# Two fused MoE layers behind block attention: token tiles scaled a step after they are summed, an early activation for the first slice of layer two, and a last slice finished on VectorE

## The chip, the cores and the metric

The kernel runs on one core of one Trainium2 chip. The metric is the device time of one execution in microseconds. The profile shows one such execution on five engines: PE (TensorE, matrix products; PEld is its weight load), DVE (VectorE), ACT (ScalarE), POOL (GpSimd) and SP, whose queue issues every transfer of this kernel.

## The reference

```python
attn = softmax(q k^T / 8, masked by blocks of 64) @ v     # 4 x 8 heads, 576 tokens, 64 wide
x = attn as 2304 tokens x 512
h = x @ w_in;   g = h * clip(h + 3, 0, 6) / 6;   x = g @ w_out          # layer one: 512 -> 2048 -> 512
h = x @ w_in2;  g = h * tanh(softplus(h));       out = g @ w_out2       # layer two
```

Everything is in single precision. The kernel makes each product of three matrix products over a high and a low part of its operands (high x high, high x low, low x high), so every operand of TensorE is first split in two.

## The kernel before, in words

**Stages.** Attention comes first, over 16 pairs of heads. Then the two layers run as one list of 160 steps, `steps` (L806): layer `m` (0, 1), token block `j` (four of 512 tokens and one of 256), slice `f` (16 slices of 128 of the 2048 inner columns). Step n makes slice n. Block 0 of layer one is steps 0 to 15, block 1 begins at step 16; layer two begins at step 80; the last slice is step 159. Below, "in 12" is `ff_in` of slice 12 (12 matmuls, L275 to L277), "out 12" is `ff_out` of slice 12 (12 matmuls, L773 to L775), and so on for other operations.

**Order.** The schedule is manual: each engine runs its instructions in the order in which the Python loop at L916 calls the stages, and waits only where its data or a buffer is not ready. In step n the loop runs through the three lists of `MOE_PLAN` (L60): list 0 for steps of block 0, list 1 for the other steps of layer one, list 2 for layer two. An entry `("out", 2)` means that step n calls out of slice n - 2.

**One slice of layer one.** `in` writes h in PSUM (two buffers); `act_a` (ACT L285) takes relu(h + 3); `act_c3` (DVE L331) multiplies by h and so frees h; `act_gh` (ACT L349) rounds the result to its high part gh; `act_gl` (POOL L356) subtracts to get the low part gl; `out` uses gh (L773, L775) and gl (L774). In layer two the activation is longer: `a` (ACT L287), `b1` (DVE L294), `b2` (DVE L301), `ln` (ACT L306), `c3` (DVE L336), `rexp` (ACT L314), `c1` (DVE L318), `c2` (DVE L324), `mul` (POOL L343), `gh`, `gl`.

**Token tiles.** Each block's input comes in four tiles k = 0 to 3 of 128 x 512. For layer one, `load_x` (L224) issues on SP: raw (`xr`, two buffers), low (`xs`, one buffer), rs (`xn`, one buffer, two transfers). Then `add_x` sums raw and low (POOL L245), `mul_x` scales by rs (DVE L250), and `split_x` makes the high part xh (ACT L257) and the low part xl (DVE L262), after which raw's buffer is free. The steps in which these run, counted from the block's first step, are the tuples `XLOAD`, `XADD` and `XSPLIT` at L102: their first entry is for block 1, the second for the later blocks of layer one, the third for layer two. `xa`, `xm`, `xh`, `xl` and `dma` are their places in a plan.

**Beside it in block 0.** Up to step 13 the weights of the later slices are still being converted: per step two rebases on ACT (L163), two signs on POOL (L168), two merges L182 and two L185 on DVE, two copies on ACT (L202), and one subtraction on POOL and one on DVE (L207).

**The turns.** At step 80 the outs of layer one's last slices (256 tokens) are called at lag 2 and those of layer two at lag 3, so TensorE's order is in 80, out 79, in 81, in 82, in 83, out 80, in 84, out 81. At the end it is out 158, out 159, then `evacuate` and the last stores.

Of the kernel before, what the change touches and what calls it, by code (L numbers as in the profile page):

```python
# [25 lines left out]
FT = DFF // P  # L26
# [4 lines left out]
BLOCKS = [(t, min(512, NT - t)) for t in range(0, NT, 512)]  # L31
# [28 lines left out]
MOE_PLAN = (  # L60
    (
        ("evac", 3), ("c3", 1), ("w0", 0), ("w1", 0), ("gh", 1), ("gl", 1), ("xh", 0), ("in", 0),
        ("w2", 0), ("w3", 0), ("a", 0), ("out", 2), ("whi", 0), ("dma", 0), ("wlo", 0), ("xl", 0),
        ("xa", 0), ("xm", 0),
    ),
    (
        ("evac", 3), ("c3", 1), ("gh", 1), ("gl", 1), ("xh", 0), ("w0", 0), ("in", 0), ("out", 2),
        ("w1", 0), ("w2", 0), ("w3", 0), ("xl", 0), ("a", 0), ("whi", 0), ("dma", 0), ("wlo", 0),
        ("xa", 0), ("xm", 0),
    ),  # L70
    (
        ("evac", 4), ("in", 0), ("out", 3), ("a", 0), ("gh", 2), ("gl", 2), ("b1", 0), ("b2", 0),
# [26 lines left out]
RELOAD = 4  # L99


XLOAD = (-7, -4, -3, -2), (-11, -9, -6, -3), (-11, -9, -9, -6)  # L102
XADD = (-5, -4, -3, -2), (-10, -8, -5, -2)
XSPLIT = (-4, -3, -2, -1), (-9, -7, -4, -1), (-10, -8, -7, -1)
END = 0


def f32(ap):
    return ap.bitcast(F32)
# [7 lines left out]
def fused_kernel(ctx: ExitStack, tc: tile.TileContext, qT, kT, vv, w1, w2, outT):  # L117
    nc = tc.nc
# [147 lines left out]
    ht, et, qt, rt, gt = {}, {}, {}, {}, {}  # L266
# [73 lines left out]
    def act_mul(m, j, f):  # L340
        if m == 1:
            g, _ = gt[m, j, f]
            nc.gpsimd.tensor_mul(g, g, et.pop((m, j, f)))  # L343

    def act_gh(m, j, f):
        n = BLOCKS[j][1]
# [5 lines left out]
    def act_gl(m, j, f):  # L352
        n = BLOCKS[j][1]
        g, gh = gt[m, j, f]
        gl = m3.tile([P, 512], F32R, tag="gl", name=f"gl{m}_{j}_{f}")[:, :n]
        nc.gpsimd.tensor_sub(gl, g, f32(gh))  # L356
        gt[m, j, f] = gh, gl


    with ExitStack() as late:  # L360
# [271 lines left out]
        def stage(fn):  # L632
            def run(g):
                if 0 <= g < NG:
                    fn(g // 5, TIME[g % 5])
            return run

        def stage_v(fn):

            def run(g):  # L640
                p, c = divmod(g - 5, 5)
                if 0 <= p < NP and c < 4:
                    fn(p, c // 2, c % 2)
            return run

        def stage_sums(t):
            def run(g):
                p, s = divmod(g, 5)
                if 0 <= p < NP and s == 4:
                    sums(p, t)  # L650
            return run

        def stage_q(t):
            def run(g):
                p, s = divmod(g, 5)
                if 0 <= p < NP - 1 and s == t:
                    split_q(p + 1, t)
            return run
# [36 lines left out]
        def stage_fetch(g):  # L695
# [4 lines left out]
        stages = dict(  # L700
            load=stage_load, loadv=stage_load_v, T=stage(transposes), hi=stage(keep_hi), lo=stage(keep_lo),
            max=stage(maxima), exp=stage(exps),
            rg=stage_sums(0), rt=stage_sums(1), rc=stage_sums(2), rd=stage_sums(3),
            S=stage(scores), V=stage_v(attn_v), x=stage_v(keep_x), store=stage_v(store_x),
            qh=stage_q(0), ql=stage_q(1), qd=stage_q(2), pool=stage_pool, w=stage_w, fetch=stage_fetch,
        )


        begun = set()
        conv0 = {}  # L710

        def run_early(name, f, *args):
            if name == "load":
                load_x(0, 0, f)
            elif name == "add":
                add_x(0, 0, f)
            elif name == "mul":
                mul_x(0, 0, f)
            elif name in ("xh", "xl"):
                split_x(0, 0, f, name == "xl")  # L720
            elif name == "fetch":
                fetch1(f, *args)
            elif name == "conv":
                c, i = args
                if i == 0:
                    conv0[f, c] = weights1(f, c)
                next(conv0[f, c], None)
            else:
                begun.add((name, f))
                fn = dict(a=act_a, c3=act_c3, gh=act_gh, gl=act_gl)  # L730
                fn["in"] = ff_in
                fn[name](0, 0, f)
# [52 lines left out]
    def put(d, n, *call):  # L785
        d.setdefault(n, []).append(call)
# [15 lines left out]
            dst = x2d[d] if m == 0 else outT[d * P:(d + 1) * P]  # L802
            put(results, now[0], nc.sync.dma_start, dst[:, t0:t0 + n], o)

    NJ = len(BLOCKS)
    steps = [(m, j, f) for m in range(2) for j in range(NJ) for f in range(FT)]  # L806

    conv, dmas, stores, loads, results = {}, {}, {}, {}, {}  # L810
    xs = {}, {}, {}, {}
# [29 lines left out]
    for n, (m, j, f) in enumerate(steps):  # L841
        if m == 0 and j == 0 and f >= WMID:
            for c in range(2):
                put(conv, n - 3, weights1_psum, f, c)
                put(dmas, max(n - AHEAD, 0), fetch1, f, c, True)
        if m == 0 and 1 <= j <= 2:
            i = (j - 1) * FT + f
            put(dmas, n - 2, fetch2, i)
            put(conv, n, narrow2, i)
        if (m, j) == (0, NJ - 1):  # L850
            put(dmas, n + RELOAD, reload2, f)
        if f == 0 and n:
            when = 2 if m else min(j - 1, 1)
            for k in range(KT):
                put(loads, n + XLOAD[when][k], load_x, m, j, k)
                i = n + XSPLIT[when][k]
                if m == 0:
                    put(xs[0], n + XADD[when][k], add_x, m, j, k)
                    put(xs[3], n + XADD[when][k], mul_x, m, j, k)
                put(xs[1], i, split_x, m, j, k, 0)  # L860
                put(xs[2], i, split_x, m, j, k, 1)

    now = [0]
    active = {}

    def group(n):
# [9 lines left out]
    def calls(*ds):  # L876
        def run_stage(n, m):
            if m == group(n):
                for d in ds:
                    for fn, *args in d.pop(n, ()):  # L880
                        fn(*args)
        return run_stage
# [7 lines left out]
    def conv_step(i):  # L890
        def run_stage(n, m):
            if m != group(n):
                return
            if m == 0:
                todo = begin(n) if i == 0 else active.get(n - (i == 5), ())
            elif i == 1:
                todo = begin(n + 1)
            else:
                if i == 0 and n not in active:
                    for x in begin(n):  # L900
                        next(x)
                todo = active[n]
            for x in todo:
                next(x, None)
        return run_stage

    stages = dict(
        a=stage(act_a), b1=stage(act_b1), b2=stage(act_b2), ln=stage(act_ln),
        rexp=stage(act_rexp), mul=stage(act_mul), c1=stage(act_c1), c2=stage(act_c2),
        c3=stage(act_c3), gh=stage(act_gh), gl=stage(act_gl), evac=stage(evacuate),  # L910
        out=stage(ff_out), dma=calls(results, stores, dmas, loads), xa=calls(xs[0]), xh=calls(xs[1]), xl=calls(xs[2]), xm=calls(xs[3]),
        w0=conv_step(0), w1=conv_step(1), w2=conv_step(2), w3=conv_step(3),
        whi=conv_step(4), wlo=conv_step(5),
    )
    stages["in"] = stage(ff_in)
    for n in range(len(steps) + 6):  # L916
        now[0] = n
        for i, plan in enumerate(MOE_PLAN):
            for name, lag in plan:
                if (name, n - lag) not in begun:  # L920
                    stages[name](n - lag, i)
    assert not (dmas or loads or results or stores or conv or any(xs))


# [37 lines left out]
```

## Time and profile before

| | us |
|---|---|
| median of 3 runs (1016.84 to 1017.82) | 1017.66 |
| the profiled execution | 1016.85 |
| its span in the profile | 1014.3 |
| TensorE busy in the span | 985.6 |

The median is 0.81 us above the profiled execution. The span leaves 2.55 us of that execution outside. Times of single instructions below are counted from the start of the span. A row of a timeline reads: start, duration, engine and line, operation, output<-input, shape, and in brackets how long the engine stood idle just before and what ended that.

### The profile page before, as it was taken

To read this page: it belongs to the slowest core of one execution; us is meant where nothing else is said; L and a number is where in the kernel's file an instruction comes from. 1 tells how busy PE (TensorE), PEld (TensorE's weight loads), DVE (VectorE), ACT (ScalarE), POOL (GpSimd) and SP (SyncE) were. 2 spreads that over 40 slices of the span, in tenths; PEclk is the share of its full clock that TensorE was granted. 3 is DMA by queue.
4 is the path that set the end of the run, shared out by engine and by line. 5 is a ranking of instruction groups with operands and counts; after the bars stand their busy time and mean duration, and the time that the engine had idled before them with its cause. 6 is when DMAs were issued, how large, how long until landed. Compare 5 with 4: busy or idle time off the path is not lost.

```text
span 1014.3 us, 14797 instructions
## 1 busy us (share of the span) xinstructions
PE 985.6 (97%) x5184; PEld 842.9 (83%) x5184; DVE 618.7 (61%) x1039; ACT 517.0 (51%) x1175; POOL 583.5 (58%) x510
## 2 busy tenths in 40 slices
PE   6999999989989999999999999999999999999998
PEld 5888899868768888888888997888888888888897
DVE  6888877958856556654222226556656566656575
ACT  4788888846535445444222334445444444444454
POOL 7555544568967787776222223655555565555644
PEclk9999999999999999999999999999999999999999
DMA  6677677788037677674110595000200100100010
GB/s 177 171 200 207 174 187 193 195 284 334 14 112 262 231 256 254 212 248 156 63 31 11 211 392 186 22 1 1 73 11 1 63 21 1 41 18 6 1 42 21
DMA packets 95641, 128.89 MB, mean 127 GB/s; under 512 B 42320, under 2 KB 54608, under 8 KB 95568
## 3 DMA queue, kind: packets, MB, share of 16 engines
q1 hardware_dynamic: 95568, 127.96, 39.5%
q8 instruction: 40, 0.66, 0.3%
q14 instruction: 33, 0.27, 0.1%
HBM read 83.36 MB, written 35.73 MB: 117 GB/s over the span
## 4 chain that ended last, share of the span: by engine, by line
PE 75%; POOL 9%; issue 5%; DVE 4%; DMA 4%; ACT 3%; SPq 1%; POOLq 0%; DVEq 0%; ACTq 0%
PE y L774 11%; PE y L775 11%; PE h L276 11%; PE h L277 11%; PE h L275 11%; PE y L773 11%; PE o L606 3%; POOL gl L356 3%; PE t L576 2%; POOL wl L207 2%; PE s L503 2%; DMA qb<-qs 1%; PE s L504 1%; PE s L505 1%; POOL hq L343 1%
## 5 line engine op out<-in xcount | busy, mean ns | idle before, releaser
L275 PE MATMUL h<-xh,wh 128*128 128x512 f32 (+1 forms) x640 | 237.0, 370 | 4.9 <-DVE e L331 3.0
L774 PE MATMUL y<-gl,wh 128*128 128x512 f32 (+1 forms) x640 | 236.0, 369 | 2.9 <-POOL gl L356 2.9
L277 PE MATMUL h<-xh,wl 128*128 128x512 f32 (+1 forms) x640 | 236.4, 369 | 1.3 <-POOL wl L207 1.3
L773 PE MATMUL y<-gh,wh 128*128 128x512 f32 (+1 forms) x640 | 235.8, 368 | 0.7 <-ACT gh L349 0.7
L276 PE MATMUL h<-xl,wh 128*128 128x512 f32 (+1 forms) x640 | 236.0, 369 | 0.4 <-DVE xl L262 0.4
L775 PE MATMUL y<-gh,wl 128*128 128x512 f32 (+1 forms) x640 | 235.4, 368 | 0.0
L356 POOL TENSOR_TENSOR gl<-e,gh 128x512 fp32r<-128x512 f32 (+1 forms) x80 | 105.5, 1319 | 135.0 <-ACT gh L349 69.9
L356 POOL TENSOR_TENSOR gl<-hq,gh 128x512 fp32r<-128x512 f32 (+1 forms) x80 | 127.6, 1595 | 89.7 <-ACT gh L349 89.7
L343 POOL TENSOR_TENSOR hq<-hq,e 128x512 f32<-128x512 f32 (+1 forms) x80 | 99.3, 1241 | 83.4 <-DVE e L324 82.8
L275 PEld LDWEIGHTS h<-xh,wh 128*128 128x128 f32 x640 | 121.0, 189 | 27.3 <-DVE e L331 3.8
L774 PEld LDWEIGHTS y<-gl,wh 128*128 128x128 f32 x640 | 120.6, 188 | 23.9 <-POOL gl L356 4.2
L277 PEld LDWEIGHTS h<-xh,wl 128*128 128x128 f32 x640 | 121.0, 189 | 21.7 <-POOL wl L207 1.8
L773 PEld LDWEIGHTS y<-gh,wh 128*128 128x128 f32 x640 | 120.7, 189 | 21.6 <-ACT gh L349 1.7
L276 PEld LDWEIGHTS h<-xl,wh 128*128 128x128 f32 x640 | 121.2, 189 | 20.8 <-DVE xl L262 0.6
L775 PEld LDWEIGHTS y<-gh,wl 128*128 128x128 f32 x640 | 120.7, 189 | 19.9
L294 DVE TENSOR_SCALAR e<-e 128x512 f32<-128x512 f32 (+1 forms) x80 | 33.2, 415 | 144.5 <-ACT e L287 136.6
L287 ACT ACTIVATE e<-h 128x512 f32<-128x512 f32 (+1 forms) x80 | 44.4, 555 | 144.9 <-PE h L277 144.9
L331 DVE SCALAR_TENSOR_TENSOR e<-e,h 128x512 f32<-128x512 f32 (+1 forms) x80 | 50.3, 628 | 84.2 <-ACT e L285 83.9
L285 ACT ACTIVATE e<-h 128x512 f32<-128x512 f32 (+1 forms) x80 | 43.8, 548 | 105.7 <-PE h L277 105.7
L349 ACT ACTIVATE gh<-e 128x512 fp32r<-128x512 f32 (+1 forms) x80 | 46.9, 588 | 82.9 <-DVE e L331 82.9
L587 DVE TENSOR_TENSOR t<-t,t 128x512 fp32r<-128x512 f32 (+2 forms) x144 | 69.9, 522 | 26.9 <-ACT t L582 26.7
L536 ACT ACTIVATE p<-s,nm 128x64 f32<-128x64 f32 (+2 forms) x144 | 75.2, 530 | 11.9 <-DVE nm L525 11.9
(63 smaller groups left out, 1621.9 us busy)
## 6 DMA issues: line engine op xcount, KB each, us to landing
raw<-w SPq DMA_DIRECT2D x64, 512.0 KB
x1d<-x SPq DMA_DIRECT2D x64, 144.0 KB
qb<-qs SPq DMA_DIRECT2D x30, 288.0 KB
w2d<-m SPq DMA_DIRECT2D x32, 256.0 KB
w2d<-v SPq DMA_DIRECT2D x32, 256.0 KB
wh<-w2d SPq DMA_DIRECT2D x16, 512.0 KB
wl<-w2d SPq DMA_DIRECT2D x16, 512.0 KB
q<-qT SPq DMA_DIRECT2D x16, 288.0 KB
```

The source lines that it names most:

```text
L275: nc.tensor.matmul(h[:, :n], hi[:, ws], xh, start=(k == 0), stop=False)
L276: nc.tensor.matmul(h[:, :n], hi[:, ws], xl, start=False, stop=False)
L277: nc.tensor.matmul(h[:, :n], lo[:, ws], xh, start=False, stop=(k == KT - 1))
L331: nc.vector.scalar_tensor_tensor(g, g, 6.0, h, op0=ALU.min, op1=ALU.mult)
L343: nc.gpsimd.tensor_mul(g, g, et.pop((m, j, f)))
L349: nc.scalar.activation(gh, g, AF.Copy)
L356: nc.gpsimd.tensor_sub(gl, g, f32(gh))
L536: nc.scalar.activation(t, sc, AF.Exp, bias=nm[:, c:c + 1], accum_out=su[:, i:i + 1])
L587: nc.vector.tensor_sub(z[:, 1, loc, :], tp, f32(z[:, 0, loc, :]))
L773: nc.tensor.matmul(y, hi[:, ws], gh, start=first, stop=False)
L774: nc.tensor.matmul(y, hi[:, ws], gl, start=False, stop=False)
L775: nc.tensor.matmul(y, lo[:, ws], gh, start=False, stop=last)
```

## The change

Three things. For layer one, `mul_x` of a token tile is called one step after its `add_x`, from a place in the middle of the plan (ahead of `dma`) in place of its end; with that the steps of loads, sums and splits move: for block 1 the loads of tiles 1 to 3 and all four sums come a step earlier, so that the scalings stay at steps 11 to 14; for blocks 2 to 4 the sums of tiles 0 to 2 stay, tile 3 is loaded and summed a step earlier, and tiles 0 to 2 are split a step later. Slice 80, the first of layer two, has c1, c2 and mul at the end of step 80 in place of step 81, and gh and gl at the end of step 81 in place of step 82. Slice 159, the last, has mul and gl on VectorE in place of GpSimd.

```diff
@@ MOE_PLAN, list 0
-        ("w2", 0), ("w3", 0), ("a", 0), ("out", 2), ("whi", 0), ("dma", 0), ("wlo", 0), ("xl", 0),
-        ("xa", 0), ("xm", 0),
+        ("w2", 0), ("w3", 0), ("a", 0), ("out", 2), ("whi", 0), ("xm", 0), ("dma", 0), ("wlo", 0),
+        ("xl", 0), ("xa", 0),
@@ MOE_PLAN, list 1
-        ("w1", 0), ("w2", 0), ("w3", 0), ("xl", 0), ("a", 0), ("whi", 0), ("dma", 0), ("wlo", 0),
-        ("xa", 0), ("xm", 0),
+        ("w1", 0), ("w2", 0), ("w3", 0), ("xm", 0), ("xl", 0), ("a", 0), ("whi", 0), ("dma", 0),
+        ("wlo", 0), ("xa", 0),
@@
-XLOAD = (-7, -4, -3, -2), (-11, -9, -6, -3), (-11, -9, -9, -6)
-XADD = (-5, -4, -3, -2), (-10, -8, -5, -2)
-XSPLIT = (-4, -3, -2, -1), (-9, -7, -4, -1), (-10, -8, -7, -1)
+XLOAD = (-7, -5, -4, -3), (-11, -9, -6, -4), (-11, -9, -9, -6)
+XADD = (-6, -5, -4, -3), (-10, -8, -5, -3)
+XSPLIT = (-4, -3, -2, -1), (-8, -6, -3, -1), (-10, -8, -7, -1)
@@ act_mul (and act_gl in the same way)
-            nc.gpsimd.tensor_mul(g, g, et.pop((m, j, f)))
+            eng = nc.vector if (m, j, f) == steps[-1] else nc.gpsimd
+            eng.tensor_mul(g, g, et.pop((m, j, f)))
@@
-                    put(xs[3], n + XADD[when][k], mul_x, m, j, k)
+                    put(xs[3], n + XADD[when][k] + 1, mul_x, m, j, k)
@@ at the end of each step of the loop; first = NJ * FT = 80
+        for name in (("c1", "c2", "mul"), ("gh", "gl"))[n - first] if 0 <= n - first < 2 else ():
+            stages[name](first, 2)
+            begun.add((name, first))
```

## Rows read from the trace of the kernel before

**Rows 1.** The page's part 1: busy time of each engine, share, instructions.

```profile
PE 985.6 (97%) x5184; PEld 842.9 (83%) x5184; DVE 618.7 (61%) x1039; ACT 517.0 (51%) x1175; POOL 583.5 (58%) x510
```

**Rows 2.** Busy time by stretch: length; PE, PEld, DVE, ACT, POOL; clock, DMA, GB/s.

```profile
270.00:302.00 32.00, 28.61 (x122) 22.12 (x121) 19.22 (x25) 12.84 (x24) 22.31 (x18) 1.00 0.32 99
302.00:500.00 198.00, 198.00 (x875) 163.97 (x874) 111.25 (x123) 87.11 (x151) 138.26 (x109) 1.00 0.64 215
600.00:626.00 26.00, 24.70 (x151) 21.48 (x150) 12.11 (x21) 10.15 (x20) 6.22 (x7) 1.00 0.64 235
1003.00:1014.30 11.30, 6.36 (x45) 5.35 (x43) 3.50 (x9) 2.82 (x7) 3.80 (x6) 0.96 0.14 46
```

**Rows 3.** Timeline, steps 12 to 16: a tile's sum, its scaling, c3 12, TensorE.

```profile
281.88 1.74 POOL L245 TENSOR_TENSOR xr<-xr,xs 128x512 f32<-128x512 f32 x1
283.65 0.69 DVE L250 TENSOR_TENSOR xr<-xr,xn 128x512 f32<-128x512 f32 x1 [1.18 <-POOL xr L245]
284.26 0.68 DVE L331 SCALAR_TENSOR_TENSOR e<-e,h 128x512 f32<-128x512 f32 x1
284.99 0.50 PE L275 MATMUL h<-xh,wh 128*128 128x512 f32 x1 [1.44 <-DVE e L331]
...
298.41 0.50 PE L774 MATMUL y<-gl,wh 128*128 128x512 f32 x1 [0.91 <-POOL gl L356]
...
301.08 0.39 PE L275 MATMUL h<-xh,wh 128*128 128x512 f32 x1
```

**Rows 4.** Timeline, step 10: VectorE's two merges L182 beside GpSimd's gl 9.

```profile
264.89 2.83 DVE L182 SCALAR_TENSOR_TENSOR v<-raw,v 128x512 uint32<-128x512 uint32 x2 [1.34 <-POOL v L168]
265.43 1.75 POOL L356 TENSOR_TENSOR gl<-e,gh 128x512 fp32r<-128x512 f32 x1
```

**Rows 5.** Timeline and one stretch: loads, what frees their buffer, when they land.

```profile
191.86 0.33 SPq L233 DMA_DIRECT2D xs<-x1d  x1
194.88 1.27 POOL L245 TENSOR_TENSOR xr<-xr,xs 128x512 f32<-128x512 f32 x1 [1.16 <-DMA xs<-x1d]
...
276.03 0.33 SPq L233 DMA_DIRECT2D xs<-x1d  x1
276.90:278.20 1.30, 0.80 (x4) 0.34 (x3) 1.30 (x3) 0.41 (x1) 0.77 (x1) 1.00 0.65 200
280.68 1.78 DVE L262 TENSOR_TENSOR xl<-xr,xh 128x512 fp32r<-128x512 f32 x1
282.49 0.33 SPq L232 DMA_DIRECT2D xr<-x1d  x1
285.68 1.29 POOL L356 TENSOR_TENSOR gl<-e,gh 128x512 fp32r<-128x512 f32 x1 [2.07 <-ACT gh L349]
```

**Rows 6.** Timeline, the turn to layer two: b1 81, mul 80, b1 82, out 80, gl 81.

```profile
617.41 0.43 DVE L294 TENSOR_SCALAR e<-e 128x512 f32<-128x512 f32 x1 [2.31 <-ACT e L287]
620.68 1.29 POOL L343 TENSOR_TENSOR hq<-hq,e 128x512 f32<-128x512 f32 x1 [11.61 <-DVE e L324]
621.18 1.07 DVE L294 TENSOR_SCALAR e<-e 128x512 f32<-128x512 f32 x1
622.70 0.50 PE L773 MATMUL y<-gh,wh 128*128 128x512 f32 x1 [0.32 <-ACT gh L349]
624.18 0.50 PE L774 MATMUL y<-gl,wh 128*128 128x512 f32 x1 [0.98 <-POOL gl L356]
627.26 1.30 POOL L356 TENSOR_TENSOR gl<-hq,gh 128x512 fp32r<-128x512 f32 x1 [0.74 <-ACT gh L349]
```

**Rows 7.** Timeline, the end: xl at 256 columns, c2 159, gl 158, out 159.

```profile
954.50 0.42 DVE L262 TENSOR_TENSOR xl<-xr,xh 128x256 fp32r<-128x256 f32 x1
1005.46 0.42 DVE L324 SCALAR_TENSOR_TENSOR e<-e,r 128x256 f32<-128x256 f32 x1
1006.44 0.72 POOL L356 TENSOR_TENSOR gl<-hq,gh 128x256 fp32r<-128x256 f32 x1 [0.53 <-ACT gh L349]
1009.17 0.39 PE L774 MATMUL y<-gl,wh 128*128 128x256 f32 x1 [0.25 <-POOL gl L356]
```

More of the change, by code (lines that the diff above doesn't have):

```diff
@@ L355, in act_gl @@
         gl = m3.tile([P, 512], F32R, tag="gl", name=f"gl{m}_{j}_{f}")[:, :n]
-        nc.gpsimd.tensor_sub(gl, g, f32(gh))
+        eng = nc.vector if (m, j, f) == steps[-1] else nc.gpsimd
+        eng.tensor_sub(gl, g, f32(gh))
         gt[m, j, f] = gh, gl
+    NJ = len(BLOCKS)
+    steps = [(m, j, f) for m in range(2) for j in range(NJ) for f in range(FT)]
     with ExitStack() as late:
@@ L803, in evacuate @@
             put(results, now[0], nc.sync.dma_start, dst[:, t0:t0 + n], o)
-    NJ = len(BLOCKS)
-    steps = [(m, j, f) for m in range(2) for j in range(NJ) for f in range(FT)]
     conv, dmas, stores, loads, results = {}, {}, {}, {}, {}
@@ L863, in fused_kernel @@
     now = [0]
+    first = NJ * FT
     active = {}
```

## The prediction, made before the change was run

> **What bounds the kernel now.** I read the page first: TensorE is busy for 97% of the span [rows 1], so only its gaps can be won, and a new gap is paid in full. The busy time by stretch shows where the gaps are [rows 2]. From 302 to 500 us, which holds the token tiles of blocks 2 to 4, TensorE has none: 875 matmuls in 198 us, 0.226 us each. Whatever the new order does for VectorE's waits there is worth nothing as long as it makes no gap. Three stretches have gaps that the change can reach. Steps 11 to 16 (270 to 302 us) hold 122 matmuls, 27.6 us of work at that pitch in 32 us: 4.4 us lost. The turn to layer two (600 to 626 us) has 1.3 us idle; the matmul starts say more: 0.32 us waited ahead of out 80, then 1.48 us between its first two starts where 0.23 is usual, and each matmul after a wait runs 0.1 us longer [rows 6], together 1.8 us. The last 11.3 us hold 45 matmuls, but most of that is the final stores, which stay.
>
> Next the timeline of steps 12 to 16 [rows 3]. The loss there is one pattern, seen four times: VectorE stands still for a sum on GpSimd (until 283.65), scales, and only then does c3, which frees the buffer that the next slice waits for (TensorE starts at 284.99 after 1.44 us). The change takes the scaling away from this place. The question is what comes late next.
>
> **Part one, block 1's token tiles.** Instructions are neither added nor removed: four sums on GpSimd and the loads of tiles 1 to 3 come a step earlier; the scalings stay in steps 11 to 14, but ahead of the step's L207 and xl.
>
> *Steps 10 to 12.* GpSimd and VectorE get in each other's way here: beside GpSimd's gl, two merges L182 take 2.83 us, with one run before gl and the other after it, and gl itself takes 1.75 us, where it takes 1.29 alone [rows 4, 5]. So the sum that now comes in step 10, ahead of step 11's weight conversions, pushes both engines: 1.27 us for the sum [rows 5]. In step 12 gl 11 comes to lie between the two merges, as in [rows 4] (0.6 us, the second merge's wait, net of what it waited before), and the scaling of tile 1 now runs ahead of xl 0 (0.69 us). xl 0, which ends at 282.46 now (280.68 and 1.78), ends some 2.5 us later, at about 284.9. Bounds: not later at all (if the earlier sum fits in a gap), and 3 us.
>
> *The load that is held.* Raw has two buffers, so raw 2 can't be loaded before xl 0 is through: SP issues it at 282.49, 0.03 us after xl 0 [rows 5]. Before, sum 2 stands one step after xl 0, and nobody sees the load. After the change load 2, xl 0 and sum 2 are all in step 12 (16 - 4), and load 3, xl 1 and sum 3 all in step 13. GpSimd, in order, stands at sum 2 until raw 2 and its low part have landed, and behind that sum stand gl 12, for which out 12 on TensorE waits, the subtraction of step 13, and sum 3. On VectorE, scaling 2 stands ahead of xl 1 and c3 13.
>
> Price of a held load: 0.03 to the issue, about 0.45 to the issue of low (an issue takes 0.33), and the landing. The trace has low at 3.0 us from issue to the sum that waited for it, beside heavy traffic (191.86 to 194.88). With the queue quiet, the low issued at 276.03 moves its 256 KB from 276.9 to 278.2 (1.3 us at 200 GB/s), so it lies there 2.2 us after its issue [rows 5]. Here the queue is quiet: I take 2.35, and keep 3.0 as the far end. So a hold is 2.83 us.
>
> *The chain.* From the end of xl 0: hold 2.83, sum 2 1.26, gl 12 1.27 (queued behind the sum, it goes ahead of the scaling), scaling 2 0.65, subtraction 1.25, L207 0.6, xl 1 0.65: 8.5 us, so xl 1 ends at about 293.4. Again: hold 2.83, sum 3 1.26, gl 13 1.27, scaling 3 0.65, xl 2 0.65, c3 14 0.65, then gh 14 0.7 and gl 14 1.3: 9.3 us, gl 14 at 302.7, out 14's first use of it at 302.8. In the kernel before that same matmul starts at 298.41 and in 16 follows at 301.08 [rows 3]. So in 16 comes at about 305.5: **4.4 us later**. The pieces are as in [rows 3 to 5]; gh is ACT's 0.63 and a hand-over. With xl 0 at its old time the chain still gives +1.9; with xl 0 3 us late and two landings of 3.0, +6.2.
>
> *Blocks 2 to 4.* Loads, sums, scalings and splits are a step or more apart there, and each load of raw comes after the split that frees its buffer. xn waits for the scaling of the same step, which now runs ahead of the load; nobody waits for it for more than a step. Their cover is a TensorE that has no gap for 198 us [rows 2]. Cost nothing; were the cover gone, a late sum would cost what GpSimd's gl loses, up to 1 us each.
>
> **Part two, slice 80.** c1 and c2 (0.69 each) fit into the 2.31 us in which VectorE waits for b1 81, ended at 617.41. The product (1.29 on GpSimd) then starts at about 617.2 in place of 620.68 [rows 6], gh and gl follow after the step's other work, and out 80 finds both: the 1.8 us go. But b1 82 beside that product took 1.07 us in place of 0.43: it stood until GpSimd was done [rows 6]. The product now meets b1 81, holds it until 618.5, and b2 and c3 81 with it; c3 81 frees the buffer of in 83, which had no slack: 0.95 us back. Then in 84 and out 81 come 0.9 us earlier, while gl 81 comes not earlier but some 0.7 us later (ScalarE now has gh 80 ahead of a 82): gl 81 ends at 628.56 before and would at 629.25; out 81 wants it at 629.73 before, 24 matmuls after 624.18, and would at 628.8: 0.55 us back. Net **0.3 us gained**. Bounds: 1.8 gained if nothing collides, 0.5 lost if out 81 waits longer.
>
> The Trainium skill (SBUF — State Buffer, "Who interferes with whom") says of this that VectorE and GpSimd share a pair of ports, that the one that begins first holds it for its whole instruction, and that a VectorE instruction with at most one SBUF input outside the fast modes doesn't take part. The trace agrees: 1.07 against 0.43. If the two could run side by side, part two would give 1.2 to 1.3 us in place of 0.3; that alone would not change the sign below.
>
> **Part three, slice 159.** On VectorE a two-operand instruction of 256 columns takes 0.42 us [rows 7]; GpSimd's takes 0.72. c2 159 ends at 1005.88, the product is done by 1006.35, gh 159 by 1006.85 behind gh 158, and gl 159 stands behind GpSimd's gl 158 (1006.44 to 1007.16) and ends at 1007.6. Out 159's second matmul, at 1009.17 with 0.25 us waited and a late start, comes right behind the first: **0.5 us gained**. At worst the product delays gl 158 by 0.3 and that is lost. The stores behind it stay as they are.
>
> **The sum.** +4.4 - 0.3 - 0.5 = +3.6 us. The profiled execution has 1014.3 in the span and 2.55 around it, 1016.85; it would become 1020.45. The median of the runs, 1017.66, lies 0.81 above it, so I predict a median of **1021.3**. Its own range: 1.9 - 1.8 - 0.5 gives 1017.3; 6.2 + 0.5 + 0.3 gives 1024.7.
>
> **The rivals.** *The untied scaling wins.* VectorE no longer stands still for a sum, and the four waits go. For it: [rows 3]. Against it: the held load, which needs xl 0 to end at about 280.5 or sooner to cost nothing; it ends at 282.46 already now. It decides if raw 2 is issued before GpSimd is through with step 12. If then only the crowding of steps 10 to 12 stays (in 13 and in 14 wait some 3 us), part one gives -1.5 and the whole 1015.3; if that goes too, -4.4 and with the other two 1012.5. *A draw.* xl 0 keeps its old time and the held load costs 1.9, less 0.8 from the others: 1018.8; or part two gives its full 1.8: 1017.3. For it: GpSimd is only 70% busy in this stretch (22.31 of 32) [rows 2], so that the earlier sum might find room. *The change does little of what it says:* in block 1 the scalings stay in their steps and only sums and loads move, so what is gained over the sum on one side is asked of the load on the other; that is the forecast's own reason.
>
> **How the numbers follow.** Forecast, slower by more than 2 us: 0.60. Draw: 0.20. The untied scaling wins: 0.20. A measurement of this kernel can tell about 0.2% (2 us) from no change. The range takes in forecast and draw and ends at 1015.0 and 1024.5; what is left out is most of the winning rival and the forecast's upper end.
>
> **What would show it.** Right: sum 2 and sum 3 with idle time ended by a transfer of raw or low, raw 2 issued right behind xl 0 at 284 or later, out 12 and out 13 waiting for gl by 1 us or more, in 16 at about 305. For part two: b1 81 of about 1 us, no wait of out 80, a wait of out 81. For part three: out 159 without a wait. Wrong: GpSimd never waiting for a load in steps 12 and 13, or xl 0 before 281.

## The result, and the profile after the change

| | before | after |
|---|---|---|
| median of 6 runs each (range) | 1017.0 us (1015.03 to 1017.82) | 1021.34 us (1019.97 to 1024.66) |
| ratio, 95% interval | | 1.0052 (1.0039 to 1.0064) |
| the profiled execution, its span | 1016.85, 1014.3 | 1021.14, 1019.4 |

The changed kernel is 0.5% slower, 5.3 us by the ratio. The predicted median was 1021.3.

To see where it went, three stretches are measured from one matmul's start to another's, so that a shift of the whole trace drops out:

| stretch | before | after | difference | forecast |
|---|---|---|---|---|
| in 10 to in 16 (token tiles of block 1) | 40.25 | 44.94 | +4.69 | +4.4 |
| in 80 to in 85 (the turn to layer two) | 22.66 | 22.44 | -0.22 | -0.3 |
| out 158 to the last matmul | 4.05 | 3.55 | -0.50 | -0.5 |
| sum | | | +3.97 | +3.6 |

The span grew by 5.1 us. The other 1.1 us are already there when in 10 starts, at 261.93 in the trace after and 260.83 before, ahead of everything that the change moves. In the profiles of all kernels of this study, that start lies anywhere from 260.1 to 262.9. It is scatter of single executions; a time of after below is compared with one of before after taking 1.10 us off.

The page's part 1 of after answers to [rows 1]: the same matmuls, 39 us more busy time on VectorE.

```profile
PE 987.4 (97%) x5184; PEld 844.6 (83%) x5184; DVE 657.6 (65%) x1041; ACT 516.8 (51%) x1175; POOL 588.7 (58%) x508
```

Busy time by stretch of after (length; PE, PEld, DVE, ACT, POOL; clock, DMA, GB/s) answers to [rows 2], with the first bound moved to 306 us, so that it holds step 15's end:

```profile
270.00:306.00 36.00, 29.43 (x119) 22.57 (x118) 22.78 (x26) 13.32 (x25) 20.81 (x17) 0.95 0.27 88
306.00:500.00 194.00, 194.00 (x858) 160.63 (x857) 144.51 (x122) 86.11 (x150) 144.86 (x109) 1.00 0.65 220
500.00:600.00 100.00, 100.00 (x557) 87.79 (x556) 22.13 (x36) 27.83 (x55) 27.13 (x28) 1.00 0.29 109
```

The same first two stretches of before:

```profile
270.00:306.00 36.00, 32.60 (x139) 25.46 (x138) 22.35 (x29) 14.54 (x28) 23.87 (x20) 1.00 0.32 100
306.00:500.00 194.00, 194.00 (x858) 160.63 (x857) 108.13 (x120) 85.41 (x149) 136.71 (x107) 1.00 0.65 218
```

Two things are to be seen. In the first 36 us TensorE does 119 matmuls in place of 139: here the time is lost. In the 194 us behind it VectorE is busy 36 us longer and TensorE has no gap in either kernel: that costs nothing. These 194 us hold the scalings of blocks 2 and 3 alone; the prediction counted block 4 in, but its four run between 515 and 554 us of after. TensorE has no gap there either, and from in 16 to in 80 both kernels take 308.51 us.

Now the timeline of after for steps 12 to 16, which answers to [rows 3, 5]: start, duration, engine and line, operation, output<-input, shape, and in brackets the idle time before and what ended it. (L358 is gl, L778 to L780 are out; SPq is SP's queue issuing a transfer.)

```profile
283.95 0.68 DVE L262 TENSOR_TENSOR xl<-xr,xh 128x512 fp32r<-128x512 f32 x1
...
284.65 0.33 SPq L232 DMA_DIRECT2D xr<-x1d  x1
285.08 0.38 SPq L233 DMA_DIRECT2D xs<-x1d  x1
285.28 0.50 PE L275 MATMUL h<-xh,wh 128*128 128x512 f32 x1 [0.64 <-DVE e L331]
...
288.11 1.27 POOL L245 TENSOR_TENSOR xr<-xr,xs 128x512 f32<-128x512 f32 x1 [5.32 <-DMA xs<-x1d]
289.33 1.26 POOL L358 TENSOR_TENSOR gl<-e,gh 128x512 fp32r<-128x512 f32 x1
289.64 1.50 DVE L250 TENSOR_TENSOR xr<-xr,xn 128x512 f32<-128x512 f32 x1 [4.42 <-DMA xn<-rsd]
290.65 0.50 PE L779 MATMUL y<-gl,wh 128*128 128x512 f32 x1 [2.13 <-POOL gl L358]
...
292.76 0.68 DVE L262 TENSOR_TENSOR xl<-xr,xh 128x512 fp32r<-128x512 f32 x1
...
293.47 0.33 SPq L232 DMA_DIRECT2D xr<-x1d  x1
294.10 0.50 PE L275 MATMUL h<-xh,wh 128*128 128x512 f32 x1 [0.66 <-DVE e L331]
294.22 0.31 SPq L233 DMA_DIRECT2D xs<-x1d  x1
...
297.45 1.26 POOL L245 TENSOR_TENSOR xr<-xr,xs 128x512 f32<-128x512 f32 x1 [5.17 <-DMA xs<-x1d]
298.67 1.26 POOL L358 TENSOR_TENSOR gl<-e,gh 128x512 fp32r<-128x512 f32 x1
299.31 1.17 DVE L250 TENSOR_TENSOR xr<-xr,xn 128x512 f32<-128x512 f32 x1 [5.27 <-DMA xn<-rsd]
299.99 0.79 PE L779 MATMUL y<-gl,wh 128*128 128x512 f32 x1 [2.65 <-POOL gl L358]
...
302.47 1.29 POOL L358 TENSOR_TENSOR gl<-e,gh 128x512 fp32r<-128x512 f32 x1 [2.54 <-ACT gh L350]
...
306.87 0.39 PE L275 MATMUL h<-xh,wh 128*128 128x512 f32 x1
```

This is the held load, twice. xl 0 ends at 284.63; 0.02 us later SP issues raw 2, then its low part; GpSimd stands 5.32 us until they have landed; gl 12 comes right behind sum 2, and out 12 has waited 2.13 us for it. xl 1 ends at 293.44, raw 3 is issued, and the same happens once more: 5.17 us on GpSimd, 2.65 on TensorE.

TensorE's waits of 0.4 us or more between in 12 and in 16 make the sum: 0.50, 0.64, 2.13, 0.66 and 2.65, together 6.58 us, where the same stretch of before has 0.50, 1.44, 0.55 and 0.91, together 3.40. That is 3.18 of the 4.69 us. The other 1.5 are TensorE itself, running slower: behind the last of these waits nine matmuls start in 3.42 us (299.99 to 303.41), where they take about 1.9 otherwise. Busy time by stretch of after shows why:

```profile
298.00:300.00 2.00, 0.01 (x1) 0.01 (x1) 0.69 (x1) 0.00 (x0) 1.93 (x2) 0.95 0.97 280
299.90:303.10 3.20, 3.11 (x7) 2.48 (x8) 1.99 (x4) 1.39 (x3) 0.66 (x2) 0.50 0.34 136
303.10:306.87 3.77, 3.77 (x18) 3.05 (x16) 1.81 (x2) 1.42 (x3) 1.83 (x2) 0.98 0.03 7
```

The granted clock was 0.50, the lower of its two levels (1.2 GHz), for some 3 us after the wait, and back at 0.98 from 303.1. Most of this would have been waited anyway: gl 14 ends at 303.76, and from out 14's first use of it to in 16 is 2.67 us [rows 3], which gives some 306.5. In 16 started at 306.87, so the slow clock cost an estimated 0.4 us.

The turn, timeline of after, which answers to [rows 6] (the product of slice 80, b1 81, in 83, out 80, out 81):

```profile
622.99 1.29 POOL L344 TENSOR_TENSOR hq<-hq,e 128x512 f32<-128x512 f32 x1 [8.13 <-DVE e L324]
623.20 1.37 DVE L294 TENSOR_SCALAR e<-e 128x512 f32<-128x512 f32 x1 [0.28 <-ACT e L287]
...
626.07 0.50 PE L275 MATMUL h<-xh,wh 128*128 128x512 f32 x1 [0.88 <-DVE hq L336]
...
628.96 0.39 PE L778 MATMUL y<-gh,wh 128*128 128x512 f32 x1
...
635.15 0.50 PE L779 MATMUL y<-gl,wh 128*128 128x512 f32 x1 [0.36 <-POOL gl L358]
```

Out 80 waits for nothing now. b1 81 takes 1.37 us in place of 0.43 beside the product, in 83 waits 0.88 for c3 81 behind it, and out 81 waits 0.36 for gl 81.

The end, timeline of after, which answers to [rows 7] (product and gl of slice 159 on VectorE, gl 158, out 158):

```profile
1011.49 0.43 DVE L344 TENSOR_TENSOR hq<-hq,e 128x256 f32<-128x256 f32 x1
...
1012.01 0.72 POOL L358 TENSOR_TENSOR gl<-hq,gh 128x256 fp32r<-128x256 f32 x1 [0.53 <-ACT gh L350]
1012.53 0.48 DVE L358 TENSOR_TENSOR gl<-hq,gh 128x256 fp32r<-128x256 f32 x1 [0.61 <-ACT gh L350]
1012.79 0.39 PE L779 MATMUL y<-gl,wh 128*128 128x256 f32 x1 [0.42 <-POOL gl L358]
```

gl 159 is done at 1013.01, 0.28 us after gl 158, and out 158's wait for gl 158 is TensorE's last: out 159 has none.

### The profile page after: what moved, and what is told of

Same layout as the page of the kernel before. It is cut to its first block, busy times and chain, and to the rows that moved or that the text cites. A ratio compares the mean times of both kernels' runs of the same rounds, so it can differ in the third digit from the quotient of the medians.

```text
span 1019.4 us, 14809 instructions
## 1 busy us (share of the span) xinstructions
PE 987.4 (97%) x5184; PEld 844.6 (83%) x5184; DVE 657.6 (65%) x1041; ACT 516.8 (51%) x1175; POOL 588.7 (58%) x508
## 4 chain that ended last, share of the span: by engine, by line
PE 78%; POOL 7%; DVE 5%; issue 3%; DMA 3%; ACT 3%; SPq 1%; POOLq 0%; DVEq 0%; ACTq 0%
PE y L779 11%; PE y L780 11%; PE y L778 11%; PE h L275 11%; PE h L276 11%; PE h L277 11%; PE o L611 3%; PE t L581 3%; POOL gl L358 2%; PE s L508 2%; POOL wl L207 2%; PE s L509 2%; PE s L510 1%; ACT p L541 1%; DMA xn<-rsd 1%
## 5 line engine op out<-in xcount | busy, mean ns | idle before, releaser
L778 PE MATMUL y<-gh,wh 128*128 128x512 f32 (+1 forms) x640 | 236.5, 369 | 0.3 <-ACT gh L350 0.3
L780 PE MATMUL y<-gh,wl 128*128 128x512 f32 (+1 forms) x640 | 236.2, 369 | 0.0
L358 POOL TENSOR_TENSOR gl<-hq,gh 128x512 fp32r<-128x512 f32 (+1 forms) x79 | 126.4, 1601 | 90.8 <-ACT gh L350 90.8
L358 POOL TENSOR_TENSOR gl<-e,gh 128x512 fp32r<-128x512 f32 (+1 forms) x80 | 110.8, 1385 | 112.7 <-ACT gh L350 73.9
L778 PEld LDWEIGHTS y<-gh,wh 128*128 128x128 f32 x640 | 121.3, 190 | 20.7 <-ACT gh L350 0.5
L780 PEld LDWEIGHTS y<-gh,wl 128*128 128x128 f32 x640 | 121.1, 189 | 20.2
L182 DVE SCALAR_TENSOR_TENSOR v<-raw,v 128x512 uint32<-128x512 uint32 x64 | 85.9, 1356 | 16.1 <-POOL v L168 16.1
```

The costliest lines, as they stand in the source:

```text
L182: nc.vector.scalar_tensor_tensor(bits, low, 29, bits, op0=ALU.logical_shift_right, op1=ALU.bitwise_or)
L358: eng.tensor_sub(gl, g, f32(gh))
L778: nc.tensor.matmul(y, hi[:, ws], gh, start=first, stop=False)
L780: nc.tensor.matmul(y, lo[:, ws], gh, start=False, stop=last)
```

## The experiments

The theory, from here on H: raw 2 and raw 3 find no free buffer before the xl of two tiles earlier is through, sums 2 and 3 stand in the same step as that xl, and GpSimd hands the wait on to gl and TensorE. The rivals: the earlier sum's crowding of steps 10 to 12 alone does it (R1), or the new order in blocks 2 to 4, with VectorE's 36 us, does (R2).

**The parts alone.** Block 1's new tuples and plan, with the later blocks left as they were before:

```diff
-                    put(xs[3], n + XADD[when][k], mul_x, m, j, k)
+                    put(xs[3], n + XADD[when][k] + (j == 1), mul_x, m, j, k)
```

> The first part of the change for block 1 alone (list 0 of the plan, the first entries of the load and sum steps, the scaling of block 1 a step after the sum). Theory H, the held load: all of the loss is here, 4 to 5 us slower than before, with GpSimd waiting some 5 us for a load ahead of sum 2 and again ahead of sum 3. Rival C, the crowding of VectorE and GpSimd in blocks 2 to 4 (VectorE 33 us more busy there after the change): within 1 us of before.

Measured: 1023.69 us (1021.29 to 1024.16) beside 1017.41, ratio 1.0058 (1.0046 to 1.007). The timeline's two sums and the out that waits longest:

```profile
288.18 1.26 POOL L245 TENSOR_TENSOR xr<-xr,xs 128x512 f32<-128x512 f32 x1 [5.41 <-DMA xs<-x1d]
...
297.76 1.26 POOL L245 TENSOR_TENSOR xr<-xr,xs 128x512 f32<-128x512 f32 x1 [5.41 <-DMA xs<-x1d]
...
300.30 0.66 PE L774 MATMUL y<-gl,wh 128*128 128x512 f32 x1 [2.90 <-POOL gl L356]
```

Block 1 alone gives the whole loss and the same two waits; by the ratio it is 5.9 us, more than the 4 to 5 expected. In 10 to in 16 is 45.82 us, 0.88 more than in after, and 0.77 of that are longer waits of TensorE (7.35 us against 6.58). Up to step 15 the two kernels are the same, so a single profile of this stretch can be off by that much.

Blocks 2 to 4 alone, with their scaling a step later (`j > 1` in the line above), and block 1 as before:

> The first part for blocks 2 to 4 alone. Theory H: no gap on TensorE from step 17 to step 79, 0 us within 1. Rival C: 3 to 5 us slower, and gaps on TensorE in blocks 2 to 4.

Measured: 1017.32 beside 1017.41, ratio 1.0 (0.9991 to 1.0009). The groups of VectorE by line, from 306 to 500 us (count, busy time and mean of one in ns, idle time before), first of this kernel:

```profile
L182 DVE SCALAR_TENSOR_TENSOR v<-raw,v 128x512 uint32<-128x512 uint32 x31 | 51.2, 1650 | 1.6 <-POOL v L168 1.6
...
L250 DVE TENSOR_TENSOR xr<-xr,xn 128x512 f32<-128x512 f32 x8 | 14.2, 1774 | 0.0
```

and of before:

```profile
L182 DVE SCALAR_TENSOR_TENSOR v<-raw,v 128x512 uint32<-128x512 uint32 x31 | 32.6, 1052 | 1.5 <-POOL v L168 1.5
...
L250 DVE TENSOR_TENSOR xr<-xr,xn 128x512 f32<-128x512 f32 x8 | 5.5, 692 | 34.2 <-POOL xr L245 34.2
```

The scaling no longer waits for its sum (34.2 us of idle time gone), but runs 1.77 us in place of 0.69, and the merges grow as well: what was waiting became contention. Neither reaches TensorE: it is busy without a gap from 306 to 600 us of this run too, which takes in block 4. R2 falls.

Slice 80 alone (the loop's last lines in the diff, and nothing else):

> The second part alone: c1, c2, product, gh and gl of slice 80 a step early. Forecast: 0.3 us faster, which can't be told from no change in the time; in the trace out 80 without a wait, in 83 waiting 0.9 us for c3 81, out 81 waiting 0.4 us for gl 81. If the port between VectorE and GpSimd did not matter: 1.2 us or more faster and b1 81 at 0.43 us.

Measured: 1016.85 beside 1017.41, ratio 0.9999 (0.9989 to 1.0009); in 80 to in 85 is 22.42 us, 0.24 less than before, b1 81 takes 1.38 us and in 83 waits 0.89.

Slice 159 alone (mul and gl of the last slice on VectorE):

> The third part alone: product and gl of slice 159 on VectorE. Forecast: 0.5 us faster, within the noise of the time; in the trace out 159 without a wait for gl and the span from the start of out 158 to the last matmul 0.5 us shorter. Rival: GpSimd's gl 158 is held by VectorE's product and the gain is below 0.2.

Measured: 1016.21 beside 1017.41, ratio 0.9988 (0.998 to 0.9997); out 158 to the last matmul is 3.54 us, 0.51 less than before. The ratio's 1.2 us holds the 0.5 in its interval; the stretch is the sharper measure.

**The held load taken away.** The change as it is, but raw 2 and raw 3 of block 1 lie in buffers of another pool that is idle then:

```diff
-        raw = xr.tile([P, 512], F32, tag="xr", name=f"xr{m}_{j}_{k}")[:, :n]
+        late = (m, j) == (0, 1) and k > 1
+        raw = (m4 if late else xr).tile(
+            [P, 512], F32, tag="o" if late else "xr", name=f"xr{m}_{j}_{k}")[:, :n]
```

> The changed kernel with raw of block 1's tiles 2 and 3 in buffers that stand empty in block 0 (those of the results), so that their loads need not wait for xl 0 and xl 1; the order of everything else is unchanged. Theory H: sum 2 and sum 3 no longer wait for a load, the waits of out 12 and out 13 for gl go, in 16 comes 5 to 7 us sooner than in the changed kernel, and the whole is 1.5 to 3 us faster than before (1014 to 1015.5). Rival D, the crowding of steps 10 to 12 alone makes the loss: 2 to 4 us slower than before, as the changed kernel.

Measured: 1015.28 us (1013.8 to 1016.31) beside 1017.06, ratio 0.9983 (0.9974 to 0.9992). The timeline has sums 2 and 3 without a wait, and TensorE's only waits of 0.4 us or more between in 12 and in 16 are for c3 (lines are two higher than in after):

```profile
278.57 0.50 PE L277 MATMUL h<-xh,wh 128*128 128x512 f32 x1 [0.98 <-DVE e L333]
...
282.41 1.83 POOL L247 TENSOR_TENSOR xr<-xr,xs 128x512 f32<-128x512 f32 x1
...
286.05 0.50 PE L277 MATMUL h<-xh,wh 128*128 128x512 f32 x1 [1.70 <-DVE e L333]
...
289.68 1.74 POOL L247 TENSOR_TENSOR xr<-xr,xs 128x512 f32<-128x512 f32 x1
...
292.62 0.50 PE L277 MATMUL h<-xh,wh 128*128 128x512 f32 x1 [0.84 <-DVE e L333]
```

in 12 to in 16 takes 28.94 us in place of 34.06: with the load free, 5.1 us come back, more than part one had cost, and the change turns from a loss to a gain. R1 falls as the cause of the loss. But of the 4.4 us that the untied scaling was meant to win, 0.4 are won (28.94 against 29.37 before), and even that is not clear of scatter: with slice 80 alone, whose block 1 is that of before, the stretch takes 28.51. What is left are 3.52 us of waits for c3. R1's crowding is in them: ahead of c3 11 and c3 12 VectorE's L207 takes 1.79 and 1.77 us beside GpSimd's sums, where it takes 0.68 in before. The third, in 15's 0.84, stands behind the scaling of tile 2, which waits 1.00 us for rs.

The same buffers in the kernel before:

> The kernel before with the same two buffers, nothing else. Theory H: in the order of before the loads have a step to spare and nobody waits for them: 0 us within 1. Rival: the buffers by themselves bring what e5 brings.

Measured: 1016.89 beside 1017.06, ratio 1.0 (0.9991 to 1.0009); in 12 to in 16 is 29.36. Before the change nobody waits for these loads, and the buffers alone are worth nothing.

One of the two loads freed, tile 3's (`k == 3` in place of `k > 1`):

> The changed kernel with the free buffer for raw of tile 3 alone, so that raw 2 still waits for xl 0. Theory H: the wait ahead of sum 2 stays (about 5 us on GpSimd), the wait ahead of sum 3 goes; about half of the loss stays, 1.5 to 3 us slower than before. Rival: one hold costs nothing, as e5; or all, as the changed kernel.

Measured: 1018.31 beside 1016.9, ratio 1.0013 (1.0004 to 1.0021); in 12 to in 16 is 31.15 us, 2.2 more than with both free and 2.9 less than with both held. Timeline:

```profile
289.55 1.26 POOL L247 TENSOR_TENSOR xr<-xr,xs 128x512 f32<-128x512 f32 x1 [5.41 <-DMA xs<-x1d]
...
292.08 0.80 PE L781 MATMUL y<-gl,wh 128*128 128x512 f32 x1 [2.21 <-POOL gl L360]
...
293.67 1.72 POOL L247 TENSOR_TENSOR xr<-xr,xs 128x512 f32<-128x512 f32 x1
```

Sum 2 waits as in after, sum 3 doesn't, and the loss in the stretch is about half. Each held load has its own price. The time, +1.4 us, lies a little below what was expected.

**Slice 80's collision taken away.** Part two alone, with the product of slice 80 on VectorE:

```diff
-            nc.gpsimd.tensor_mul(g, g, et.pop((m, j, f)))
+            eng = nc.vector if (m, j, f) in (steps[NJ * FT],) else nc.gpsimd
+            eng.tensor_mul(g, g, et.pop((m, j, f)))
```

> The second part alone with the product of slice 80 on VectorE in place of GpSimd. Theory: c1, c2 and product (0.7 us each) begin at the same place as in e3 and end 0.7 us later than c2; b1 81 is then 0.4 us late in place of 0.95, in 83 waits 0.4 us or less, and the turn (in 80 to in 85) is 0.4 to 0.6 us shorter than in e3. Rival: c3 81 is as late as in e3 since VectorE itself is the queue; no shorter.

Measured: 1015.9 beside 1017.06, ratio 0.9989 (0.9981 to 0.9998). Timeline of the product, b1 81, in 83 and out 81:

```profile
616.43 0.69 DVE L344 TENSOR_TENSOR hq<-hq,e 128x512 f32<-128x512 f32 x1
617.04 0.42 DVE L294 TENSOR_SCALAR e<-e 128x512 f32<-128x512 f32 x1
...
618.96 0.50 PE L275 MATMUL h<-xh,wh 128*128 128x512 f32 x1 [0.29 <-DVE hq L336]
...
628.09 0.50 PE L778 MATMUL y<-gl,wh 128*128 128x512 f32 x1 [0.45 <-POOL gl L357]
```

b1 81 is back at 0.42 us, in 83 waits 0.29 in place of 0.89, and the turn takes 21.86 us: 0.56 less than with the product on GpSimd and 0.80 less than before. That collision cost part two 0.56 us. It is not all that part two lost: out 81 still waits for gl 81, 0.45 us, where it waited 0.38 with the product on GpSimd.

**Towards a better version.** Both remedies together (the buffers, and the products of slices 80 and 159 on VectorE):

> e5 with the product of slice 80 on VectorE as in e7. Theory: the two are in different stretches and add up, some 2.2 us faster than before (1.7 of e5 and 0.5 of e7). Rival: no faster than e5.

Measured: 1015.29 beside 1016.9, ratio 0.9984 (0.9976 to 0.9992): 1.6 us, less than expected, and no better than the buffers alone. Its stretches do add up (28.87, 21.86 and 3.53 us; with those of before taken off, 0.50, 0.80 and 0.52 gained, 1.8 together), so the half microsecond of the turn is too little for the median of some ten runs to show.

Last, the crowding. On top of that, block 1's tiles 0 to 2 are summed and split a step later, tile 3 is loaded early, and its low part and rs have buffers of the idle pool as well:

```diff
-XLOAD = (-7, -5, -4, -3), (-11, -9, -6, -4), (-11, -9, -9, -6)
-XADD = (-6, -5, -4, -3), (-10, -8, -5, -3)
-XSPLIT = (-4, -3, -2, -1), (-8, -6, -3, -1), (-10, -8, -7, -1)
+XLOAD = (-7, -5, -4, -6), (-11, -9, -6, -4), (-11, -9, -9, -6)
+XADD = (-5, -4, -3, -3), (-10, -8, -5, -3)
+XSPLIT = (-3, -2, -1, -1), (-8, -6, -3, -1), (-10, -8, -7, -1)
@@ load_x: the buffers of low and rs (not shown)
```

> e8 with the sums of block 1 a step later (steps 11, 12, 13, 13), scalings in 12 to 14, splits in 13 to 15; low and rs of tile 3 have own buffers too and are loaded first. Theory of crowding: what is left between in 12 and in 16 in e5 (18.1 us of work in 28.9) is VectorE and GpSimd holding each other beside the weight conversions of steps 10 to 12; with one sum less there, in 12 to in 16 takes 0.5 to 1.5 us less than in e5 and the whole is as much faster than e8. Rival: step 13 becomes as crowded and nothing is won.

(The 18.1 us of work named there are a slip: nine groups of 12 matmuls at 0.227 us are 24.5.) Measured: 1013.55 us (1013.02 to 1015.09) beside 1016.9, ratio 0.997 (0.9959 to 0.9981). It is 0.3% faster than the kernel before, where the changed one is 0.5% slower. In 12 to in 16 takes 28.01 us, 0.93 less than with the buffers alone, as expected; the median is 1.7 us below that of both remedies, more than the stretch shows. The edit moves the sums and frees two more buffers at once, so which of the two brings it stays open. What is left in the timeline (lines are seven higher than in after):

```profile
284.33 0.50 PE L282 MATMUL h<-xh,wh 128*128 128x512 f32 x1 [0.86 <-DVE e L338]
...
286.51 1.59 DVE L257 TENSOR_TENSOR xr<-xr,xn 128x512 f32<-128x512 f32 x1 [2.24 <-DMA xn<-rsd]
...
292.12 0.50 PE L282 MATMUL h<-xh,wh 128*128 128x512 f32 x1 [2.06 <-DVE e L338]
```

Tile 1's scaling waits 2.24 us for rs, whose one buffer (`xn`) is free only after tile 0's scaling: again a load held by a buffer, now the third one, and TensorE's wait of 2.06 us, in 15's for c3 13, stands behind that scaling in VectorE's order. A buffer of its own for that rs was not tried.

## Why the prediction was right, step by step

**Part one.** The mechanism is the one forecast; the sizes inside the chain were not. Times of after with 1.10 us taken off:

| | forecast | measured |
|---|---|---|
| xl 0 ends | 284.9 | 283.53 |
| first hold, xl 0 to sum 2 | 2.83 | 3.48 |
| xl 1 ends | 293.4 | 292.34 |
| second hold, xl 1 to sum 3 | 2.83 | 4.01 |
| gl 14 ends | 302.7 | 302.66 |
| in 16 starts | 305.5 | 305.77 |

That gl 14 falls on the forecast to 0.04 us is luck: xl 0 came 1.37 us earlier than forecast, the two holds took 1.83 longer, and the rest of the chain was 0.5 shorter. *The crowding of steps 10 to 12 was over-sized.* It was to make xl 0 end 2.5 us later; it ended 1.07 later. The step charged the earlier sum and the second merge to VectorE as if it had no room. It had: from 272 to 276 us it was busy 1.60 us of 4.00 before, and 4.00 of 4.00 after (also from 273.1 to 277.1, the same stretch with the shift of 1.10). The rows of busy time by stretch, first of before, then of after:

```profile
272.00:276.00 4.00, 4.00 (x19) 3.32 (x18) 1.60 (x3) 2.24 (x4) 4.00 (x4) 1.00 0.00 0
```

```profile
272.00:276.00 4.00, 4.00 (x20) 3.30 (x19) 4.00 (x5) 0.85 (x3) 4.00 (x4) 1.00 0.23 66
```

*The hold was under-sized.* From the issue of low to the sum were 3.03 us (285.08 to 288.11) and 3.23 (294.22 to 297.45), where 2.35 was taken for a quiet queue and 3.0 kept as the far end. The row chosen [rows 5] was a low part whose raw had been loaded earlier; here raw is issued just ahead of low and both have to land (278 GB/s from 286 to 288 us, 247 from 294.4 to 297.4). That this is the reason was not tested. The far end was the nearer row. In the second hold SP also spent 0.75 us from raw's issue to low's, in place of 0.43. rs, issued behind both, landed last, and the scalings are shown waiting for it; that cost little, since gl, begun ahead of the scaling, holds the latter anyway: both scalings end 0.55 us after gl.

The rest of the chain, sum 1.22, gl 1.26, scaling 0.55 behind it, L207 1.70, xl 0.60, was near its forecast. Not foreseen was the slow clock, an estimated 0.4 us, more than the whole difference between 305.5 and 305.77. The rival in which the untied scaling wins was put to "raw 2 is issued before GpSimd is through with step 12", and the freed buffers met that condition: part one then gave 0.4 us by the stretch, no more than its scatter, where the rival had 1.5 with the crowding and 4.4 without. So that rival's price was too good even where its condition held.

**Part two.** Forecast 0.3 gained, measured 0.22 (0.24 alone). Out 80's waits went, as said. The collision was expected to give back 0.95 at in 83 and 0.55 at out 81; the waits there are 0.88 and 0.36, each with a late start of 0.1. The Trainium skill (SBUF — State Buffer, "Who interferes with whom") has it that of VectorE and GpSimd the one that issues first keeps the shared pair of ports for its whole instruction and the other blocks fully. By that rule, as an estimate with the 0.43 us of [rows 6], b1 81 works only when the product is done and ends at 624.71; the trace agrees within 0.14 us: the product ends at 624.28, b1 81 at 624.57.

**Part three.** Forecast 0.5, measured 0.50 in after and 0.51 alone. Product 0.43 and gl 0.48 on VectorE were taken as 0.42 each.

**Blocks 2 to 4.** Costed at nothing under a TensorE without gaps; nothing it was. The stretch that was read for it, 302 to 500 us, holds blocks 2 and 3 only; block 4 came out the same.

**The sum.** Forecast 3.6 us in the stretches, measured 3.97. That the spans differ by 5.1 is the scatter ahead of step 10; the medians differ by 4.3. That the median of after, 1021.34, meets the predicted 1021.3 so closely is luck as well: the forecast added 3.6 to 1017.66, the median of three runs, and over six runs that median is 1017.0.

## What to carry to other kernels

Before a consumer is called earlier, read which buffer its load needs and what frees that buffer: where the freeing instruction lies in the same step, the load's whole landing time becomes a wait on the consumer's engine, and everything queued there in order pays it. A wait that was hidden only because the consumer came late is not seen in the old trace; the issue of the load right behind the freeing instruction is. And a scaling that no longer waits for GpSimd's sum may meet GpSimd's next instruction instead: moved work should be costed beside what it will then run beside.

## What the runs showed of the hardware that was not expected

- The granted clock halves in the middle of a busy kernel. In after it stood at 1.00 through a wait of 2.13 us (288.5 to 290.65) and in the steps behind it, fell to 0.50 at the end of TensorE's idle stretch from 297.3 to 300 (0.95 over 298 to 300), and was 0.50 up to 303.1. With tile 3 alone freed, it was 0.50 from 292 to 294, after the wait of 2.21 us. The length of the wait alone does not decide it: with block 1 alone it was 1.00 from 288.5 to 293, through a wait of 2.21 us and behind it. In the kernel before, whose longest wait in these steps is 1.44 us, it stays at 1.00 [rows 2].
- In the two holds of after, raw and low together, 512 KB, took 3.0 and 3.2 us from the second issue until their reader started. The DMA engines had stood idle just before; with rs behind them they moved 239 GB/s from 285.5 to 288.1 us and 247 from 294.4 to 297.4.
- VectorE's two-operand instruction beside GpSimd's gl takes 1.77 us (mean of the 8 scalings of blocks 2 and 3) in place of 0.69, and the merges L182 1.65 in place of 1.05 (mean of 31). In the run of the later blocks alone these are 8.7 and 18.6 of the 36 us by which VectorE is busier over 194 us, without any effect on the end.
